# Turning block 0's attention outputs and its inputs of w1 by transposing DMAs instead of on TensorE, with a new order of all operations

## The chip, the cores and the metric

The kernel runs on one core of one Trainium2 chip. The metric is the device time of one execution in microseconds. Before the change it is 1130.92 us, the median of 3 runs that lie between 1130.49 and 1133.29. One further execution was profiled.

## The reference

Two layers, each an attention A and a mixer B, on x of 2048 rows and 512 columns:

```python
x = x + A(layernorm(x));  x = x + B(layernorm(x))      # twice, with the same weights

def A(x, wqkv, wo):       # S = 2048, H = 32 heads, Dh = 16, W = 8 keys, 2 rows apart
    q, k, v = split(x @ wqkv)
    logits = einsum(q, k at rows s, s-2, ..., s-14) * Dh**-0.5     # masked where the row is < 0
    o = softmax(logits) applied to v at the same rows
    return o @ wo

def B(x, w1, w2, w3, w4): # F = 1792
    h  = gelu(layernorm(x) @ w1)
    hs = (h's four groups of 128 columns, shifted by +1, -1, +2, -2 rows) @ w2
    x1 = x + hs
    return x1 + gelu(layernorm(x1) @ w3) @ w4
```

## The kernel before, in words

A layer's 2048 rows are cut into 4 blocks of 512, a block into 4 tiles of 128 rows. A block of a layer is a stage number n from 0 to 7 (the list `lb`; 0 to 3 are layer 0). The work on stage n is:

- `p1_quarters` (n = 0 alone) or `p1_stream(n)`: layer norm, turning the tile into `xt`, and the qkv product. A `p1_stream` is four tiles of three groups of 12 matmuls each (`mm<-wq_hl,xt`).
- `p2(n)`, as `p2_unit(n, ...)`: attention for four quarters of the features, on VectorE (DVE), ScalarE (ACT) and GpSimd (POOL). Each quarter leaves a tile `o`, which is turned into `oT` (lines 1110 to 1113).
- `p3(n)`: oT @ wo, the residual x, the layer norm (`normed`), four tiles turned into `nT` (lines 1170 to 1174), nT @ w1 in four groups of 12 matmuls, gelu, and `h`. In block 0 the wo product is made in four groups, one for each oT as it comes, that add up in four `acc` buffers (`early`); a w1 group needs all four tiles of nT.
- `p4(n)`: h @ w2, the second layer norm, turned into `x2T`; then `p5(n)`: the product with w3, gelu, and the product with w4 in 14 slices.

`small_weight` and `big_four` convert weights meanwhile. Most products are made with each fp32 factor as a high and a low fp16 half, in three matmuls (`HLS`).

A turn has two forms, each of three operations. `turn_pe` transposes four 128x128 pieces in f32 on TensorE (PE) with `ident` into a PSUM buffer `mm`; then ACT writes the high half from PSUM and DVE the low half (`split`). `turn_dma` has ACT write the high half of the tile in SBUF, DVE or POOL the low half beside it (by `OTHER`), both into an `f32` buffer, and SyncE (SP) issues one `dma_start_transpose` of 128 x 8 x 128 fp16, 256 KB. For `o`, whose halves are scaled by `c_o`, the low half on POOL is two instructions. The dictionary `BY_DMA` (line 279) says from which n on a kind of turn goes by DMA: before, p1, p2 and p3 from n = 1 on, p4 from 0 on. Block 0's turns of p2 and p3 therefore are on PE.

What sets the order is a table: `PLACES` holds one number for each of the 3597 operations, and `plan` sorts all operations by it. Each engine issues its own operations in that order (`InOrder`), SP its DMAs too, so an instruction that waits holds up everything behind it on its engine. `OTHER` lists the operations that run on their second choice of engine. Buffers are handed out in the same order. In the profile nearly all instructions carry the one line of `InOrder` (L323), so the groups are told by their tiles' names.

Of the kernel before, what the change touches and what calls it, by code (L numbers as in the profile page):

```python
# [236 lines left out]
class Graph:  # L237
# [3 lines left out]
    def __call__(self, key, alts, r=(), w=(), after=(), xfer=0.0, late=0.0):  # L241
# [30 lines left out]
        for b in o.touch:  # L272
            b.users += 1
            b.left += 1
        self.ops.append(o)
        return o


BY_DMA = {"p1": 1, "p2": 1, "p3": 1, "p4": 0}


def plan(ops, slots):


    pool = {k: list(range(len(v))) for k, v in slots.items()}
# [1150 lines left out]
```

## Time and profile before

| what | value |
|---|---|
| median of 3 runs | 1130.92 us (1130.49 to 1133.29) |
| the profiled execution | 1131.58 us, of which 1129.6 us are its span |
| PE busy | 1113.3 us, 99% of the span |
| DVE busy | 873.4 us, 77% |
| ACT busy | 639.0 us, 57% |
| POOL busy | 456.4 us, 40% |
| granted TensorE clock | 9 tenths or more in all slices |

The times of the trace are counted from the span's start. An arrow `oT<-mm,c_o` reads: written to oT, read from mm and c_o. A busy PE row counts the run of matmuls in it, with its last matmul's own end; successive rows overlap a little, so the distance of two starts is what a group takes. A bracket at a row's end is the idle time of the engine before it and what released it. `SPq` is SP's queue of DMA issues; its rows are as long as the issue takes, not the transfer. Numbers behind a DMA in the list of issues are KB each and the median time from issue to landing.

### The profile page before, as it was taken

Reading aid. Unit: us, or ns where it says so; the run is one execution under the profiler, and the core shown is the slowest. Engines: PE = TensorE matmul, PEld = TensorE weight load, DVE = VectorE, ACT = ScalarE, POOL = GpSimd, SP = SyncE. Lnnn points to the kernel's source line nnn. Section 1 sums busy time; section 2 is a strip of 40 time slices with the busy share of each in tenths; the row PEclk is TensorE's granted clock in tenths of the full one; section 3 lists DMA queues with packets and bytes.
Section 4 is the critical chain, followed back from the end, with each engine's and each line's share of the span. In section 5 each row is a group of like instructions: output and inputs, shape, how many; then the busy total and the mean of one; then the engine's idle time right before and its main releaser. Section 6 shows DMA issues by size and latency. Waiting matters only on the chain.

```text
span 1129.6 us, 15244 instructions
## 1 busy us (share of the span) xinstructions
PE 1113.3 (99%) x5236; PEld 525.5 (47%) x5236; DVE 873.4 (77%) x921; ACT 639.0 (57%) x1222; POOL 456.4 (40%) x554
## 2 busy tenths in 40 slices
PE   8999998999999999999999999999999999999998
PEld 6544444444444444444444444444444444444544
DVE  5999999989898999889889978666878898323212
ACT  5876885267753577364754555564546554655322
POOL 3857754147533470245515343446314341314000
PEclk9999999999999999999999999999999999999999
DMA  7789999988997589864799847974877766425322
GB/s 220 196 219 232 252 277 239 259 230 225 224 243 208 132 207 212 227 155 109 182 207 203 212 111 189 230 175 132 183 191 176 189 145 187 116 66 116 95 85 79
DMA packets 247101, 207.16 MB, mean 183 GB/s; under 512 B 134344, under 2 KB 188616, under 8 KB 247024
## 3 DMA queue, kind: packets, MB, share of 16 engines
q1 hardware_dynamic: 245408, 204.42, 72.1%
q10 hardware_dynamic: 1616, 1.77, 0.6%
q8 instruction: 41, 0.67, 0.3%
q14 instruction: 36, 0.29, 0.1%
HBM read 132.64 MB, written 37.87 MB: 151 GB/s over the span
## 4 chain that ended last, share of the span: by engine, by line
PE 80%; DVE 7%; issue 5%; POOL 4%; ACT 2%; DMA 2%; SPq 1%; ACTq 0%; POOLq 0%; DVEq 0%
PE mm L323 57%; PE acc L323 23%; DVE prod L323 4%; POOL small L323 1%; DVE L L323 1%; SPq L323 1%; ACT junk L323 1%; POOL g L323 1%; DMA nT<-in_A_wqkv_dram 1%; POOL prod L323 1%; DVE inv_p L323 0%; DVE g L323 0%; POOL inv_p L323 0%; DMA nT<-in_A_wo_dram 0%; ACT x L323 0%
## 5 line engine op out<-in xcount | busy, mean ns | idle before, releaser
L323 PE MATMUL acc<-w,g 128*128 128x512 f16 (+1 forms) x1260 | 307.1, 393 | 0.4 <-ACT g L323 0.4
L323 PE MATMUL mm<-nT,w 128*128 128x512 f16 (+1 forms) x1344 | 293.3, 372 | 3.2 <-issue 2.3
L323 PE MATMUL mm<-wq_hl,xt 128*128 128x512 f16 x1008 | 225.4, 379 | 3.5 <-DVE h L323 1.5
L323 PEld LDWEIGHTS <-w 128*128 128x128 f16 x1512 | 141.3, 98 | 158.3 <-issue 8.4
L323 ACT ACTIVATE mm<-mm,s_w 128x512 f32<-128x512 f32 (+1 forms) x144 | 90.1, 628 | 192.5 <-PE mm L323 192.2
L323 PEld LDWEIGHTS <-g 128*128 128x128 f16 x1176 | 114.9, 98 | 137.6 <-issue 0.2
L323 DVE TENSOR_TENSOR prod<-kv,L 128x2048 f32<-128x2048 f32 x64 | 150.4, 2350 | 7.2 <-POOL o L323 5.6
L323 PEld LDWEIGHTS <-xt 128*128 128x128 f16 x1008 | 98.4, 98 | 122.4 <-issue 5.0
L323 DVE TENSOR_REDUCE L<-prod 128x128 f32<-128x2048 f32 x64 | 146.2, 2284 | 1.2
L323 DVE TENSOR_TENSOR prod<-kv,q 128x2048 f32<-128x2048 f32 x58 | 136.6, 2355 | 7.5 <-DMA kv<-kv_d 7.0
L323 DVE TENSOR_TENSOR prod<-prod 128x512 f32<-128x512 f32 (+1 forms) x113 | 115.3, 1023 | 2.9
L323 POOL TENSOR_TENSOR small<-small,nhalf 128x1 f32<-128x1 f32 (+1 forms) x104 | 85.4, 823 | 78.9 <-ACT small L323 76.1
L323 POOL TENSOR_SCALAR small<-small 128x1 f32<-128x1 f32 x131 | 67.8, 520 | 61.5 <-ACT junk L323 25.5
L323 DVE SCALAR_TENSOR_TENSOR g<-mm,c_g,g 128x512 f16<-128x512 f32 x56 | 41.6, 745 | 60.3 <-ACT g L323 60.2
L323 PE MATMUL mm<-nT,w_hl 128*128 128x512 f16 x384 | 86.4, 379 | 0.0
L323 PE MATMUL mm<-w_hl,h 128*128 128x512 f16 x384 | 86.3, 379 | 0.0
L323 POOL TENSOR_TENSOR g<-f,g 128x512 f16<-128x512 f32 x29 | 39.4, 1362 | 89.7 <-ACT g L323 70.4
L323 PE MATMUL mm<-wo_hl,oT 128*128 128x512 f16 x336 | 74.1, 379 | 0.0
L323 POOL TENSOR_TENSOR prod<-prod 128x512 f32<-128x512 f32 (+1 forms) x20 | 30.7, 1534 | 91.5 <-DVE prod L323 88.9
L323 ACT ACTIVATE g<-mm,c_g 128x512 f16<-128x512 f32 x98 | 66.3, 686 | 2.0
L323 PEld LDWEIGHTS <-oT 128*128 128x128 f16 x426 | 41.6, 98 | 49.6 <-issue 0.6
L323 ACT ACTIVATE ev<-mm,s_kv 128x512 f32<-128x512 f32 x56 | 37.9, 682 | 40.8 <-PE mm L323 19.0
(200 smaller groups left out, 1287.5 us busy)
## 6 DMA issues: line engine op xcount, KB each, us to landing
w<-w SPq DMA_DIRECT2D x210, 256.0 KB, 3.3
kv<-kv_d SPq DMA_DIRECT2D x112, 352.0 KB, 5.3
kv_d<-ev SPq DMA_DIRECT2D x112, 128.0 KB, 3.2
w<-in_B_w_dram SPq DMA_DIRECT2D x42, 256.0 KB, 4.5
q_d<-ev SPq DMA_DIRECT2D x28, 256.0 KB, 3.7
w<-g SPq DMA_DIRECT2D x28, 256.0 KB, 4.9
q<-q_d SPq DMA_DIRECT2D x28, 256.0 KB, 4.6
x<-x SPq DMA_DIRECT2D x26, 256.0 KB, 4.8
```

Source lines behind the costliest of these rows:

```text
L323: i = f(*a, **k).ins
```

## The change

`BY_DMA` sends p2's and p3's turns by DMA from n = 0 on. With that the four turns of o into oT and the four of p3's tiles into nT of block 0 use `turn_dma`. The operations stay 3597, since both forms have three. All numbers of `PLACES` and the list `OTHER` are new; of these, a line each is shown. The new table is one line longer, so L323 is L324 in the changed program.

```diff
 PLACES = [int(k) for k in """
-18 67 19 169 24 136 0 1 4 3 13 10 14 5 21 20 33 38 27 22 2 6 7 36
+38 37 39 126 81 83 6 5 1 0 10 9 11 12 16 22 41 35 36 40 7 18 19 24
...
 OTHER = {int(k): 1 for k in """
-21 23 28 42 110 113 114 115 126 128 130 132 148 149 196 205 226 229 230 251 252 255 267 270
+21 28 30 37 44 109 111 112 113 114 124 126 128 132 149 174 196 199 221 227 229 252 254 255
...
-BY_DMA = {"p1": 1, "p2": 1, "p3": 1, "p4": 0}
+BY_DMA = {"p1": 1, "p2": 0, "p3": 0, "p4": 0}
```

PE before, from the last turn of oT to the first w1 group: `ident,o` is a turn of oT, `ident,f` and `ident,prod` are turns of nT, `wq_hl,xt` are groups of `p1_stream` (the first row of each), `acc<-wo_hl,oT` is the last wo group.

```order
L323 MATMUL mm_66<-ident,o_209 128x128 x4
...
L323 MATMUL mm_72<-wq_hl,xt_203 128x512
...
L323 MATMUL acc_211<-wo_hl,oT_218 128x512
...
L323 MATMUL mm_68<-wq_hl,xt_193 128x512
...
L323 MATMUL mm_66<-wq_hl,xt_193 128x512
...
L323 MATMUL mm_70<-ident,f_164 128x128 x4
...
L323 MATMUL mm_72<-wq_hl,xt_193 128x512
...
L323 MATMUL mm_66<-ident,f_168 128x128 x4
...
L323 MATMUL mm_68<-wq_hl,xt_203 128x512
...
L323 MATMUL mm_70<-ident,prod_191 128x128 x4
L323 MATMUL mm_66<-ident,f_176 128x128 x4
...
L323 MATMUL mm_70<-nT_198,w_hl 128x512
```

One qkv group stands between the last turn and the last wo group, and five qkv groups and four turns between that and w1. The same place on PE in the changed program:

```order
L324 MATMUL acc_212<-wo_hl,oT_216 128x512
...
L324 MATMUL acc_212<-wo_hl,oT_218 128x512
...
L324 MATMUL mm_68<-wq_hl,xt_200 128x512
...
L324 MATMUL mm_66<-wq_hl,xt_200 128x512
...
L324 MATMUL mm_72<-wq_hl,xt_203 128x512
...
L324 MATMUL mm_70<-wq_hl,xt_203 128x512
...
L324 MATMUL mm_68<-wq_hl,xt_200 128x512
...
L324 MATMUL mm_66<-wq_hl,xt_203 128x512
...
L324 MATMUL mm_70<-nT_188,w_hl 128x512
```

The last two wo groups stand side by side, and six qkv groups and no turn stand between them and w1. On SP the changed program has these rows there, from the last oT to the four transposes of nT (`xt` are p1's turns, `kv_d`, `q_d` and `x` attention's stores and loads, `w` weights):

```order
L324 DMA_TRANSPOSE oT_218<-f_167 128x8x128
L324 DMA w_183<-in_B_w_dram 128x4x128
L324 DMA_TRANSPOSE xt_200<-f_162 128x8x128
...
L324 DMA_TRANSPOSE xt_203<-f_179 128x8x128
...
L324 DMA w_172<-in_B_w_dram 128x4x128
L324 DMA_TRANSPOSE nT_188<-f_201 128x8x128
L324 DMA_TRANSPOSE nT_188<-prod_198 128x8x128
L324 DMA_TRANSPOSE nT_188<-f_175 128x8x128
L324 DMA_TRANSPOSE nT_188<-f_179 128x8x128
L324 DMA w_0_117<-g_176 128x1024
```

Before, SP had only the transposes of xt in that stretch; four of oT now stand among the work ahead of w1, and four of nT one behind another.

321 rows, old and new, of tables (OTHER, PLACES) are left out of this document.

## The prediction

> **What bounds the kernel now.** I read the page's busy line and chain first, then the busy times by stage, then the waits of TensorE (PE), then the timeline of block 0. The busy line and the chain:
>
> ```profile
> PE 1113.3 (99%) x5236; PEld 525.5 (47%) x5236; DVE 873.4 (77%) x921; ACT 639.0 (57%) x1222; POOL 456.4 (40%) x554
> PE 80%; DVE 7%; issue 5%; POOL 4%; ACT 2%; DMA 2%; SPq 1%; ACTq 0%; POOLq 0%; DVEq 0%
> ```
>
> PE is busy for 99% of the span, so PE work taken away looks like time taken away. The stages say where that holds (columns: length, then busy time of PE, its weight loads, DVE, ACT, POOL; clock; DMA share):
>
> ```profile
> 23.00:124.00 101.00, 98.61 (x426) 49.71 (x425) 98.42 (x93) 79.07 (x184) 73.59 (x74) 1.00 0.81 216
> 124.00:180.00 56.00, 53.67 (x262) 25.67 (x261) 55.25 (x71) 45.01 (x87) 35.48 (x47) 1.00 1.01 261
> 180.00:320.00 140.00, 136.17 (x588) 64.64 (x587) 130.15 (x149) 79.36 (x158) 60.48 (x68) 1.00 0.90 235
> 320.00:1095.00 775.00, 774.96 (x3680) 354.78 (x3679) 570.41 (x571) 417.53 (x752) 278.29 (x347) 1.00 0.69 167
> ```
>
> From 320 us on PE never stops. From 23 to 180 us, where the whole change lies, DVE is as full as PE: 98.42 of 101 and 55.25 of 56. Two engines bound that stage, and the DMA share is 1.01 in its second part. PE's waits from 130 to 320 us (total, times, longest):
>
> ```profile
> PE mm L323 <- issue: 2.3, 1, 2.3
> PE mm L323 <- DVE h L323: 1.5, 2, 1.3
> PE mm L323 <- ACT junk L323: 1.1, 3, 0.8
> PE mm L323 <- ACT ev L323: 0.7, 1, 0.7
> ```
>
> The 2.3 is the start of p5(0), the first large PE stage, which waits for its input x2T.
>
> **What the change removes.** One turn on PE, in the timeline, and all sixteen transposes of the four oT:
>
> ```profile
> 71.48 0.60 PE L323 MATMUL mm<-ident,o 128*128 128x128 f32 x4
> 71.92 5.34 PE L323 MATMUL mm<-wq_hl,xt 128*128 128x512 f16 x24
> L323 PE MATMUL mm<-ident,o x16: 272/273/273, 71.5 to 125.4; 128*128 128x128 f32 x16
> ```
>
> The next matmul starts 71.92 - 71.48 = 0.44 us after the turn does: a turn takes 0.44 of PE's row (each 0.273 overlaps its neighbour). Eight turns are 8 x 0.44 = 3.5 us. That is the most that PE's own work can give.
>
> **What it adds on the path.** Block 0's path, on PE:
>
> ```profile
> 125.08 0.60 PE L323 MATMUL mm<-ident,o 128*128 128x128 f32 x4
> 125.51 2.75 PE L323 MATMUL mm<-wq_hl,xt 128*128 128x512 f16 x12
> 128.10 2.75 PE L323 MATMUL acc<-wo_hl,oT 128*128 128x512 f16 x12
> 145.44 2.75 PE L323 MATMUL mm<-nT,w_hl 128*128 128x512 f16 x12
> 156.13 2.75 PE L323 MATMUL mm<-nT,w_hl 128*128 128x512 f16 x12
> 161.45 7.93 PE L323 MATMUL mm<-w_hl,h 128*128 128x512 f16 x36
> 169.22 7.95 PE L323 MATMUL mm<-wq_hl,xt 128*128 128x512 f16 x36
> 179.47 1.79 PE L323 MATMUL mm<-nT,w 128*128 128x384 f16 x10 [2.29 <-issue]
> ```
>
> A group of 12 matmuls takes 128.10 - 125.51 = 2.59. In order these are: the last turn of oT, a qkv group, the last wo group, the first and last of four w1 groups, p4(0), three more qkv groups, p5(0). Its other engines, each row from its engine's timeline:
>
> ```profile
> 123.99 0.77 POOL L323 TENSOR_TENSOR o<-prod 128x256 f32<-128x256 f32 x1 [0.67 <-DVE prod L323]
> 125.72 0.69 ACT L323 ACTIVATE oT<-mm,c_o 128x512 f16<-128x512 f32 x1 [1.36 <-PE mm L323]
> 127.23 0.74 DVE L323 SCALAR_TENSOR_TENSOR oT<-mm,c_o,oT 128x512 f16<-128x512 f32 x1
> 140.47 0.81 ACT L323 ACTIVATE prod<-x,small 128x512 f32<-128x512 f32 x1
> 160.67 0.74 DVE L323 SCALAR_TENSOR_TENSOR h<-mm,c_h,h 128x512 f16<-128x512 f32 x1
> ```
>
> So the last o is ready at 123.99 + 0.77 = 124.76, the last oT at 127.97, the last normalized tile of p3(0) at 140.47 + 0.81 = 141.28, the last h at 161.41. The turns that replace PE's already run in later blocks; their steps by group (busy, mean ns):
>
> ```profile
> L323 ACT ACTIVATE f<-o,c_o 128x512 f16<-128x512 f32 x23 | 16.4, 717 | 26.9 <-DVE o L323 13.4 <-POOL o L323 9.9 <-DMA w<-w 3.5
> L323 DVE SCALAR_TENSOR_TENSOR f<-o,c_o,f 128x512 f16<-128x512 f32 x14 | 12.2, 868 | 12.7 <-ACT f L323 12.7
> L323 POOL TENSOR_TENSOR f<-o,f 128x512 f16<-128x512 f32 x9 | 12.9, 1432 | 0.8
> L323 POOL TENSOR_SCALAR o<-o,c_o 128x512 f32<-128x512 f32 x10 | 11.0, 1098 | 37.4 <-ACT f L323 31.0 <-ACT prod L323 6.5
> L323 ACT ACTIVATE f<-f 128x512 f16<-128x512 f32 x45 | 28.2, 627 | 1.0
> L323 DVE TENSOR_TENSOR f<-f,f 128x512 f16<-128x512 f32 x27 | 18.3, 687 | 10.9 <-ACT f L323 10.8
> ```
>
> and their transposing DMA, on SP's timeline and as the median from issue to landing:
>
> ```profile
> 125.63 1.28 SPq L323 DMA_TRANSPOSE xt<-f  x1
> 176.14 1.28 SPq L323 DMA_TRANSPOSE nT<-prod  x1
> oT<-f SPq DMA_TRANSPOSE x23, 4.8
> ```
>
> The row at 176.14 feeds p5(0), which starts at 179.47: 3.33 us from the start of the issue to the use. I take 3.33, since that row lies nearest in time and has the same size; 4.8 is the upper end; the lower is the 1.28 of the issue alone.
>
> - Last oT (halves on ACT and DVE in the new code): 124.76 + 0.72 + 0.87 + 3.33 = 129.7. With four turns gone PE would be there at 128.10 - 4 x 0.44 = 126.3, so it now waits about 3.4 us. Behind that wait stand all later PE groups, and behind this DMA on SP one load and the next xt, issued at about 126.4 + 1.28 + 0.5 and landed 3.33 later, 131.5, before PE needs it at 129.7 + 2.6 = 132.3.
> - x, statistics and normalizing take 141.28 - 128.10 = 13.2 from the start of the last wo group, now to 142.9. The last turn of nT adds 0.63 + 0.69 + 3.33 = 4.65: nT at 147.6. PE, after the wo group and six qkv groups (7 x 2.59 = 18.1) and some tiny matmuls, comes at 148.0, so nT just fits. w1 starts at 148.0, where it was 145.44.
> - The four w1 groups stand together now: 4 x 2.59 to 158.4. The last h came 161.41 - 158.72 = 2.7 after the last w1 group: 161.1, and p4(0) at 161.2 (was 161.45). p5(0) comes 179.47 - 161.45 = 18.0 later: 179.2. So 0.3 is won, and PE, 3.5 us lighter, waits at the last wo and again at x2T.
>
> Behind p5(0) PE's remaining work is the same in both orders. Of the 4 to 6 us of waits there, the 1.5 for h may shrink, as DVE has about 1 us less to do for the turns (two lo halves go to POOL, 1.10 + 1.43 each, where POOL has 35.48 of 56): between 0 and 1.5, I take 0.5. ACT's halves change by under 0.05 each (0.69 to 0.72): nothing.
>
> The Trainium skill, page "VectorE: DVE Perf Modes", section "The three transpose paths", gives 390 ns for a 128x128 transpose on TensorE and 1309 ns on the DMA crossbar, and its section "Rules for kernel authors" prefers TensorE wherever PSUM will do as the destination. That speaks against this change. The trace agrees in direction (0.44 against 3.33), but here the engine that the rule prefers has no idle time after 320 us. By the page's 1.31 the last oT would land at 127.7 and PE alone would set the start of w1, 146.0; p5(0) at 177.2 would then make 1131.58 - 2.3 - 0.5 - 0.66, about 1128.1.
>
> **SP.** Eight issues of 1.28 are 10.2 us more on SP's queue, four of them (5.1) ahead of the last oT. SP's largest idle times from 60 to 145 us, by what they waited for:
>
> ```profile
> SPq L323 <- POOL small L323: 2.8, 2, 1.6
> SPq L323 <- ACT f L323: 2.5, 5, 0.6
> SPq L323 <- ACT junk L323: 1.4, 2, 0.9
> SPq L323 <- ACT ev L323: 1.4, 2, 0.8
> ```
>
> These alone are 8.1 us, more than the 5.1, but they are waits in order at the head of the queue, so not all can be filled. I take them as enough; the other end is a rival.
>
> **Sum.** 1131.58 (profiled execution; the median of the runs is 1130.92, 0.66 less) - 0.3 - 0.5 = 1130.8; to the median, 1130.1. A measurement of this kernel can tell about 0.3% from no change, 3.4 us: 1127.5 to 1134.3 is "the same".
>
> **The rivals.**
> 1. *PE alone sets it* (faster). If the new order brings the last o and the layer norm earlier, so that no wait replaces the turns, 3.5 stay won, with the 0.5 behind: 1126.9 (1125.9 with all 1.5). For it: PE's 99%. Against it: DVE's 98.42 of 101 and 55.25 of 56 allow some 3.3 us in all. 0.20.
> 2. *Slow landing*. Both turns land after 4.8, not 3.33: last oT at 131.2, nT at 142.9 + 1.5 + 0.63 + 0.69 + 4.8 = 150.5, p5(0) 31.2 later (179.2 - 148.0) at 181.7, or +2.2: 1133.1. For it: the DMA share of 1.01. Against: the row of 3.33 lies in that stage. 0.13.
> 3. *SP's queue* (slower). If SP's idle takes up none of the four issues ahead of the last oT, it lands 5.1 later, 134.8; w1 then starts at 134.8 + 18.3 = 153.1, p5(0) at 184.3, or +4.8: 1135.7. It decides for slower once more than about 3.5 of the 5.1 is not absorbed. For it: SP's issues stand nearly end to end there. Against: the 8.1 of idle. 0.22.
>
> That the turns don't move is excluded: the changed program has eight transposing DMAs more on SP ahead of p4(0), and eight rows less on PE.
>
> **How the numbers follow.** The saving given back as waits has 0.45, at 1130.1, with 1128 to 1132.5 as its own range (DVE's 0 to 1.5, and 1 to 2 us at the landing). The range reaches from 1126.5 (most of rival 1) to 1136.0 (past the middle of rival 3) and leaves out about 0.18. Faster: rival 1, 0.20. Slower: rival 3, 0.22. The rest, 0.58, is the same.
>
> **What would show it.** Right: PE's busy sum about 3.5 lower; a PE wait of 2 to 4 us for a DMA into oT at the last wo group near 130; w1 near 148; p5(0) near 179, again after a wait of over 2 us; nothing waiting after 320. Wrong: no wait at the last wo group and p5(0) by 177 (rival 1); oT transposes on SP issued more than 3 us after their lo half, and p5(0) past 182 (rival 3); or new waits in p2 and p5 behind 180 us, of which the order alone tells no price.

## The result, and the profile after

The changed kernel takes 1144.6 us (median of 4 runs, 1144.09 to 1148.45) beside 1131.82 for the kernel before in the same comparisons (4 runs): ratio 1.012, 95% interval 1.0094 to 1.0146. It is slower by 12.8 us; forecast were 1130.1 us, 1126.5 to 1136.0. The profiled execution has 1144.62 us, its span is 1142.4.

The busy line of the changed kernel:

```profile
PE 1116.9 (98%) x5204; PEld 524.4 (46%) x5204; DVE 881.5 (77%) x911; ACT 637.2 (56%) x1230; POOL 484.3 (42%) x559
```

PE has 32 matmuls less, and yet is busy for longer: 1116.9 against 1113.3. The turns took 8 x 0.44 = 3.5 us with them, so some 7.1 us of busy time were added: the same matmuls took longer (those of `mm<-nT,w` with 384 columns 326 ns on the mean before, 345 after). PE's idle time rose from 1129.6 - 1113.3 = 16.3 to 25.5, by 9.2. That is the whole account: - 3.5 + 7.1 + 9.2 = 12.8. By stage (columns as in the stage rows of the prediction; the last three are clock, DMA share and GB/s):

```profile
23.00:124.00 101.00, 96.04 (x394) 47.32 (x393) 98.13 (x94) 75.74 (x179) 69.64 (x70) 0.97 0.85 216
124.00:180.00 56.00, 50.63 (x229) 22.60 (x228) 50.35 (x63) 43.05 (x87) 45.12 (x47) 0.97 1.04 252
180.00:320.00 140.00, 133.63 (x567) 63.45 (x566) 124.66 (x140) 78.28 (x158) 69.22 (x80) 0.98 0.95 236
320.00:1095.00 775.00, 773.64 (x3664) 353.63 (x3665) 587.42 (x572) 419.63 (x762) 292.32 (x343) 1.00 0.68 170
```

All but some 1.3 us of the added idle time lies before 320 us, and the granted clock, 1.00 in all four stages before, is 0.97 to 0.98 there. PE's waits from 130 to 320 us:

```profile
PE mm L324 <- DMA nT<-f: 5.8, 2, 4.0
PE acc L324 <- DMA w<-in_B_w_dram: 2.0, 2, 1.1
PE acc L324 <- DMA oT<-f: 1.2, 1, 1.2
PE mm L324 <- DMA xt<-prod: 1.0, 1, 1.0
```

and the longest one before 130, which the kernel before does not have:

```profile
PE mm L324 <- ACT w_hl L324: 4.0, 1, 4.0
```

All but 0.5 us of the waits from 130 to 320 us are for a DMA now. The marks of the forecast, on PE's timeline (last wo group, first w1 group, p4(0), p5(0)):

```profile
134.18 2.76 PE L324 MATMUL acc<-wo_hl,oT 128*128 128x512 f16 x12 [1.23 <-DMA oT<-f]
155.03 11.98 PE L324 MATMUL mm<-nT,w_hl 128*128 128x512 f16 x48 [1.86 <-DMA nT<-f]
169.57 7.93 PE L324 MATMUL mm<-w_hl,h 128*128 128x512 f16 x36
190.43 6.56 PE L324 MATMUL mm<-nT,w 128*128 128x384 f16 x24 [3.98 <-DMA nT<-f]
```

Forecast were 129.7, 148.0, 161.2 and 179.2: late by 4.5, 7.0, 8.4 and 11.2 us. The rest of the span, from p5(0) on, is 1142.4 - 190.43 = 952.0, where 1129.6 - 0.8 - 179.2 = 949.6 were forecast: 2.4 more.

### The profile page after: what moved, and what is told of

Read it like the earlier page. It is cut to its first block, busy times and chain, and to the rows that moved or that the text cites. A ratio compares the mean times of both kernels' runs of the same rounds, so it can differ in the third digit from the quotient of the medians.

```text
span 1142.4 us, 15185 instructions
## 1 busy us (share of the span) xinstructions
PE 1116.9 (98%) x5204; PEld 524.4 (46%) x5204; DVE 881.5 (77%) x911; ACT 637.2 (56%) x1230; POOL 484.3 (42%) x559
## 4 chain that ended last, share of the span: by engine, by line
PE 75%; POOL 4%; ACT 3%; DMA 3%; DVE 3%; issue 1%; SPq 1%; POOLq 0%; DVEq 0%; ACTq 0%
PE mm L324 51%; PE acc L324 24%; POOL small L324 2%; DVE prod L324 1%; DMA w<-in_B_w_dram 1%; SPq L324 1%; DMA kv_d<-ev 1%; ACT f L324 1%; ACT junk L324 1%; DMA nT<-f 1%; POOL g L324 1%; DMA w<-w 0%; DVE f L324 0%; POOL o L324 0%; ACT mm L324 0%
## 5 line engine op out<-in xcount | busy, mean ns | idle before, releaser
L324 PE MATMUL acc<-w,g 128*128 128x512 f16 (+1 forms) x1260 | 307.2, 394 | 2.0 <-DMA w<-in_B_w_dram 2.0
L324 PE MATMUL mm<-nT,w 128*128 128x512 f16 (+1 forms) x1344 | 296.7, 375 | 4.4 <-DMA nT<-f 4.0
L324 PE MATMUL mm<-wq_hl,xt 128*128 128x512 f16 x1008 | 227.4, 383 | 4.4 <-ACT ev L324 1.3
L324 PEld LDWEIGHTS <-w 128*128 128x128 f16 x1512 | 142.2, 98 | 162.2 <-issue 12.1
L324 ACT ACTIVATE mm<-mm,s_w 128x512 f32<-128x512 f32 (+1 forms) x144 | 89.7, 628 | 202.3 <-PE mm L324 202.0
L324 PEld LDWEIGHTS <-g 128*128 128x128 f16 x1176 | 114.8, 98 | 137.6
L324 DVE TENSOR_TENSOR prod<-kv,L 128x2048 f32<-128x2048 f32 x64 | 150.5, 2354 | 11.8 <-POOL o L324 6.9
L324 PEld LDWEIGHTS <-xt 128*128 128x128 f16 x1008 | 99.4, 99 | 127.0 <-issue 8.6
L324 DVE TENSOR_TENSOR prod<-kv,q 128x2048 f32<-128x2048 f32 x58 | 138.9, 2396 | 12.4 <-DMA kv<-kv_d 8.9
L324 DVE TENSOR_REDUCE L<-prod 128x128 f32<-128x2048 f32 x64 | 146.1, 2282 | 1.1
L324 DVE TENSOR_TENSOR prod<-prod 128x1024 f32<-128x1024 f32 (+2 forms) x117 | 128.9, 1107 | 6.9 <-ACT prod L324 4.2
L324 POOL TENSOR_TENSOR small<-small,nhalf 128x1 f32<-128x1 f32 (+1 forms) x104 | 93.6, 903 | 82.4 <-ACT small L324 79.9
L324 POOL TENSOR_SCALAR small<-small 128x1 f32<-128x1 f32 (+1 forms) x120 | 59.7, 500 | 88.2 <-ACT junk L324 58.7
L324 PE MATMUL mm<-nT,w_hl 128*128 128x512 f16 x384 | 87.6, 384 | 1.9 <-DMA nT<-f 1.9
L324 PE MATMUL mm<-w_hl,h 128*128 128x512 f16 x384 | 85.6, 379 | 0.0
L324 DVE SCALAR_TENSOR_TENSOR g<-mm,c_g,g 128x512 f16<-128x512 f32 x56 | 41.5, 745 | 56.2 <-ACT g L324 56.1
L324 POOL TENSOR_TENSOR g<-f,g 128x512 f16<-128x512 f32 x34 | 50.1, 1480 | 73.5 <-ACT f L324 59.8
L324 PE MATMUL mm<-wo_hl,oT 128*128 128x512 f16 x336 | 74.0, 379 | 0.0
L324 ACT ACTIVATE g<-mm,c_g 128x512 f16<-128x512 f32 x98 | 65.9, 684 | 1.8
L324 PEld LDWEIGHTS <-oT 128*128 128x128 f16 x426 | 41.4, 98 | 51.2 <-DMA oT<-f 1.7
L324 PEld LDWEIGHTS <-w_hl 128*128 128x128 f16 x384 | 37.8, 99 | 48.5 <-issue 2.5
L324 PEld LDWEIGHTS <-h 128*128 128x128 f16 x384 | 37.6, 98 | 44.6
```

What stands on the lines that cost most here:

```text
L324: i = f(*a, **k).ins
```

## The experiments

Theory A: the turns themselves cost, by the landing of their DMAs and by SP's queue. Theory B: the new order costs, whichever engine turns. All times are medians of 4 to 10 runs; ratios are to the kernel before in the same comparison.

**Turns or order.** Four kernels separate them: the old order with all eight turns by DMA, the new order with them on PE, the old order with oT's turns alone, and with nT's alone.

```diff
 # e1 (before.py); e4 changes only "p2", e18 only "p3"
-BY_DMA = {"p1": 1, "p2": 1, "p3": 1, "p4": 0}
+BY_DMA = {"p1": 1, "p2": 0, "p3": 0, "p4": 0}
 # e2 (after.py)
+for _k, _v in ((404, 286.6), (405, 286.7), (406, 286.8), (415, 400.6),
...
+    PLACES[_k] = _v
-BY_DMA = {"p1": 1, "p2": 0, "p3": 0, "p4": 0}
+BY_DMA = {"p1": 1, "p2": 1, "p3": 1, "p4": 0}
```

> The order of before is kept, number for number, and the eight turns of block 0 go by DMA: each turn's three operations take the three places of the old turn. Theory A (the turns cost: the landing of each DMA, and SP's queue): the loss comes with the turns alone, so this is above 1140 us. Theory B (the new order costs: the loads of w1 stand late on SP, PE waits 4.0 us for them near 82 to 86 us, and the clock falls to 0.50 after each long wait): without the new order there is no such wait, and this is between 1130 and 1138 us, the upper end because wo follows each turn closely in this order.

Measured: 1154.81 us, ratio 1.0204 (1.0189 to 1.0219).

> The order of the changed kernel, with the eight turns of block 0 back on TensorE; the three operations of a turn stand together, near the place of the first one, because only four PSUM buffers are there. Theory A (turns cost): most of the 12.8 us comes back, 1130 to 1135 us. Theory B (order costs): the wait of 4.0 us for w1's sum of squares and the slow clock behind it stay, so 1138 to 1146 us.

Measured: 1161.64 us, 1.0265 (1.025 to 1.028).

> The order of before, with the four turns of o into oT by DMA and those of nT on TensorE. Theory A: about half of the loss, 1136 to 1140 us, since these turns are on the path once for the last oT. Theory B: 1130 to 1135 us.

Measured: 1144.64 us, 1.0119 (1.0102 to 1.0136).

> The order of before, with the four turns of nT by DMA and those of o on TensorE. If the costs of the two kinds of turn add up (e1 cost 23.2 us, e4 alone 13.0), 1140 to 1143 us. If they don't add (one long wait hides another), 1144 us or more, or under 1138.

Measured: 1142.35 us, 1.0098 (1.0083 to 1.0113).

Theory B falls: in the old order the turns alone cost 23.2 us, and the two kinds add up (13.0 + 11.1 = 24.1). Theory A as stated falls as well: the new order without its DMA turns is the slowest of all (though e2 also moves the three operations of each turn together and takes two entries out of `OTHER`, so it is not the order alone). The new order fits the new turns and takes back 1154.8 - 1144.6 = 10.2 us of what they cost in the old one. What they cost there is on PE's list of waits of e1, up to 320 us:

```profile
PE mm L323 <- DMA nT<-f: 9.2, 1, 9.2
PE mm L323 <- DMA xt<-f: 8.9, 4, 5.2
PE acc L323 <- DMA oT<-f: 4.0, 1, 4.0
```

Only 13.2 of these 22.1 us are for the newly turned tiles. The other 8.9 are for xt, p1's tiles, whose turns were by DMA already: they now stand behind the new ones on SP. The kernel before waited 0.7 for them.

**SP's queue by itself.** The kernel before, with small stores that nobody waits for at the eight places; 16 of them in e5, 32 in e17; in e16 16, with 16 loads of x issued by ACT.

```diff
 # e5 and e16; e17 has range(32) and range(4)
+    spare = [dram.tile([P, 64], F16, name=f"spare{k}") for k in range(16)]
+    EXTRA = (406, 417, 459, 470, 992, 1002, 1012, 1022)
     for o in plan(op.ops, slots):
         o.fn()
+        if o.seq in EXTRA:
+            for _ in range(2):
+                Y.dma_start(spare.pop(), wq.t[:, :64])
 # e16, e6, e7 (in dma2, used by load_x for blocks 2 and 3)
-                Y.dma_start(out(par), in_(par))
+                (q or Y).dma_start(out(par), in_(par))
```

> The kernel before, with its turns on TensorE, and 16 small stores of a part of wq_hl to spare DRAM, which nobody waits for, two at each of the eight places where an old turn had its last operation. They add SP issues alone (16 of 0.5 to 0.6, some 9 us; what the eight transposing DMAs add is 10.2), and no landing that anything needs. Theory SP (SP's queue is full from 60 to 160 us, and each issue put in delays all that stand behind it): 1137 to 1145 us. Theory landing (the path is longer because the turned tiles land later): within 3 us of before.

Measured: 1138.66 us, 1.0065 (1.0042 to 1.0088).

> The kernel before with 32 spare issues, four at each of the eight places, 17.5 us of SP. Theory SP full: each us of issue costs what it cost in e5 (6.8 for 8.8) or more, since there is no slack left: 1144 to 1150 us. If SP still had room and e5 met one unlucky place: under 1142 us.

Measured: 1147.36 us, 1.0145 (1.013 to 1.016).

> The kernel before with the 16 spare issues of e5 on SP, and 16 loads of x off SP, issued by ACT. SP's queue is then about as long as before. Theory SP (length of the queue): the loss of e5 goes, 1130 to 1134 us. Theory place (each spare issue delays what stands right behind it, and the loads taken off stood elsewhere): 1136 us or more.

Measured: 1138.18 us, 1.0058 (1.0041 to 1.0075).

Issues alone cost 0.65% for 8.8 us of SP and 1.45% for 17.2: 7.4 and 16.4 us, some 0.8 to 0.95 us for each us of issue, with no landing that anybody needs. The stores' own data, 16 KB each, did not fill the DMA engines: their busy share from 60 to 180 us is 0.94 in the kernel before, 0.92 in e5 and 0.86 in e17. (In the changed kernel it is 0.99; whether its transfers also slow each other down, these runs don't separate.) PE's wait for xt shows the way, in the kernel before, in e5 (its profiled execution is its slowest, 1143.37 us) and in e17:

```profile
PE mm L323 <- DMA xt<-f: 0.7, 1, 0.7
```

```profile
PE mm L323 <- DMA xt<-f: 4.7, 4, 2.9
```

```profile
PE mm L323 <- DMA xt<-f: 6.9, 5, 3.1
PE mm L323 <- ACT ev L323: 4.1, 3, 2.2
```

The second row of e17 is next in the line: ACT waits for buffers of ev, which SP's stores empty. From 40 to 180 us ACT waits in the kernel before, and in e17:

```profile
ACT ev L323 <- DMA kv_d<-ev: 4.4, 3, 3.0
ACT ev L323 <- DMA q_d<-ev: 2.4, 1, 2.4
```

```profile
ACT ev L323 <- DMA kv_d<-ev: 9.2, 6, 3.3
ACT ev L323 <- DMA q_d<-ev: 6.9, 4, 3.3
```

e16 says that it isn't the length of the queue: with as much taken off it as was put on, the loss stayed. That leaves the place: an issue ahead of a transfer on the path delays that transfer, and room made elsewhere is not passed on. Tile by tile this is not shown for e16: its wait for xt is only 1.7 us, yet its p4(0) starts at 167.95, 6.5 later than in the kernel before.

**Taking work off SP.**

> The changed kernel, with the loads of x for p1 of blocks 2 and 3 (8 operations, 16 issues of 0.6, 9.6 us) issued by ACT in place of SP, at the same places of the order. Theory SP: the 9.6 us come off the full queue, and most of the loss comes back: 1132 to 1139 us. Theory landing: SP's length matters little, 1142 us or more. ACT takes the issues in (75.74 of 101 us busy).

Measured: 1146.75 us, 1.0138 (1.0117 to 1.016).

> The kernel before with the same 16 issues by ACT. If SP's queue has the whole say, there is a gain here as well, at most the 6 us that PE waits from 124 to 320 us: 1126 to 1131 us. If SP only counts once it is overfull, no change within 2 us.

Measured: 1132.24 us, 1.0003 (0.9993 to 1.0013).

The loads of x were no part of the path in either kernel: neither gained. In e6 the last wo group starts at 134.22, where it started at 134.18.

**The slow clock.** In e8 warm-up matmuls fill three of PE's waits.

```diff
+    BUSY = {157: 30, 1026: 16, 1088: 30}
     for o in plan(op.ops, slots):
+        for _ in range(BUSY.get(o.seq, 0)):
+            T.matmul([t for t in o.touch if t.kind == "mm"][0].t[:, :2 * P], warm[:, :P], warm, start=True, stop=True)
         o.fn()
```

> The changed kernel with 30, 16 and 30 matmuls of warm-up data (128x256, results overwritten) on PE ahead of the three matmuls at which it idles longest (w1's sum of squares, first w1 group, p5(0)); they need nothing, so they run within the idle time. If the slow clock behind each long wait is lost time of its own: no 0.50 in the granted clock there, and 3 to 7 us less, 1138 to 1142 us. If the time that the slow clock takes is made up by shorter waits behind it: within 2 us of 1144.6.

Measured: 1141.24 us, 1.0083 (1.0064 to 1.0101); the interval still touches that of the changed kernel, though each of its four runs is faster than each of the four there. The granted clock of the changed kernel at the first of these waits and the third (length, PE busy ... clock, DMA share):

```profile
82.00:86.00 4.00, 0.58 (x3) 0.09 (x1) 3.97 (x4) 1.48 (x1) 3.92 (x3) 1.00 0.75 238
86.00:90.00 4.00, 3.42 (x9) 1.54 (x10) 4.00 (x4) 3.93 (x9) 4.00 (x4) 0.54 0.93 232
90.00:94.00 4.00, 4.00 (x13) 1.51 (x12) 4.00 (x3) 0.56 (x2) 4.00 (x2) 0.61 0.87 231
190.00:194.00 4.00, 3.57 (x12) 1.70 (x13) 3.97 (x2) 1.12 (x1) 2.16 (x2) 0.50 1.02 267
194.00:198.00 4.00, 4.00 (x17) 2.08 (x16) 3.86 (x5) 2.02 (x4) 0.00 (x0) 0.81 1.05 314
```

and of e8, at the same places of its own timeline:

```profile
86.00:88.00 2.00, 2.00 (x22) 1.81 (x20) 1.58 (x1) 2.00 (x5) 2.00 (x2) 1.00 0.79 262
88.00:90.00 2.00, 2.00 (x13) 0.98 (x12) 1.72 (x3) 1.94 (x5) 2.00 (x3) 1.00 1.03 202
194.00:196.00 2.00, 2.00 (x14) 1.23 (x13) 1.90 (x4) 1.71 (x3) 0.00 (x0) 1.00 1.02 333
```

At 0.54, 0.61, 0.50 and 0.81 the 16 us of these rows lose some 4 x (0.46 + 0.39 + 0.50 + 0.19) = 6.2 us; with the shorter spell behind the wait ahead of w1 this is about the 7.1 of the account above. With PE kept busy the clock stays at 1.00 at these places, and about half of that comes back (3.4). PE's waits for xt are 6.2 us in e8, where they were 2.0, though 1.98 of that stands ahead of the first warm-up and can't come from it. The third warm-up also cost time of its own: it ran to 192.14, though the last turn ahead of p5(0) was issued at 186.26 and so was due near 189.5, by the 3.26 us from issue to use in the changed kernel (an estimate).

**Single delays on the path.** The changed kernel's last o comes at 128.07 and not at 124.76, with two halves of oT ahead of it on POOL; the last of w1's four loads stands behind the first turn on SP (78.09, the load 79.68, its use 84.52); a weight's low half stands ahead of a root of p4(0). Each was taken away alone.

```diff
 # e3: two loads of w1 behind the second one        # e10: the weight's half behind the root
+for _k, _v in ((154, 272.3), (153, 272.6)):        +for _k, _v in ((267, 742.5),):
+    PLACES[_k] = _v                                 +    PLACES[_k] = _v
 # e9: seqs 416 and 458 out of OTHER
-... 413 414 416 458 463 467 473
+... 413 414 463 467 473
```

> The changed kernel with two of the four loads of w1 moved ahead on SP, to stand behind the second one; nothing else. Theory A: SP's queue and the landings of the turns set the later path anyway, so this stays within 3 us of 1144.6. Theory B: the wait of 4.0 us before the sum of squares of w1 and the some 3 us of slow clock behind it go, and with them 4 to 7 us: 1137 to 1141 us.

Measured: 1147.22 us, 1.0133 (1.0101 to 1.0164).

> The changed kernel with the two low halves of oT that OTHER puts on POOL (1.64 + 1.47 us there, the later pair ahead of the last o) back on DVE (0.87 each). Theory POOL (the last o comes at 128.07 and not at 124.76, since POOL's queue holds it up): last o some 2 to 3 us earlier, last wo group at 131 to 132 in place of 134.18, and 2 to 4 us less: 1141 to 1143 us. Theory SP (the transposes would wait on SP's queue anyway): last wo group within 1 us of 134.18, 1144 to 1147 us.

Measured: 1142.83 us, 1.0107 (1.0082 to 1.0133).

> The changed kernel with one low half of a weight (POOL, w and g, 179.26 to 183.15) moved behind p4(0)'s last layer norm on POOL. Theory POOL: the root that waits for it comes some 2 us earlier, PE idles 2 us less ahead of p5(0), below the length that brings the clock to 0.50, so p5(0) at 188 to 189 in place of 190.43 and 3 to 5 us less: 1140 to 1142 us. Theory SP: no change beyond 2 us.

Measured: 1145.32 us, 1.011 (1.009 to 1.0131).

None is told from no change. Two of them show why. In e3 the wait ahead of w1's sum of squares fell from 4.00 to 1.17 us, but PE's wait for an xt just before it grew from 0.97 to 3.23, since that xt's turn is issued behind the two loads, at 75.41 and not at 73.28:

```profile
79.77 5.35 PE L326 MATMUL mm<-wq_hl,xt 128*128 128x512 f16 x24 [3.23 <-DMA xt<-f]
```

e9's POOL has the last o two us earlier (124.44 + 1.52 = 125.96; it was 126.22 + 1.85):

```profile
124.44 1.52 POOL L324 TENSOR_TENSOR o<-prod 128x256 f32<-128x256 f32 x2
```

Its DVE has the low half at 128.86:

```profile
128.11 0.75 DVE L324 SCALAR_TENSOR_TENSOR f<-o,c_o,f 128x512 f16<-128x512 f32 x1 [0.89 <-ACT f L324]
```

But SP comes to that turn at 131.42 (130.95 in the changed kernel):

```profile
126.11 0.93 SPq L324 DMA_DIRECT2D kv_d<-ev  x1
127.15 0.54 SPq L324 DMA_DIRECT2D q<-q_d  x1
128.16 2.65 SPq L324 DMA_DIRECT2D kv_d<-ev  x4
130.85 0.47 SPq L324 DMA_DIRECT2D kv_d<-x  x1
131.42 1.30 SPq L324 DMA_TRANSPOSE oT<-f  x1
```

and PE at 134.63, where it was 134.18:

```profile
134.63 2.76 PE L324 MATMUL acc<-wo_hl,oT 128*128 128x512 f16 x12 [1.54 <-DMA oT<-f]
```

Six stores and one load stand between the third and the fourth turn on SP, and the tile waits 2.6 us for them.

**Several at once, and shorter issues.** e11 is e9 and e10 together, e12 adds e8's warm-up; e13 is e9 and e6, e14 is all four; e15 has plain copies for the eight transposing DMAs, so that block 0's oT and nT aren't turned.

> Both edits, the low halves on DVE and the weight's low half behind the root. Theory POOL: the sum of the two, 1137 to 1140 us. Theory SP: 1142 us or more.

Measured: 1145.35 us, 1.0117 (1.0093 to 1.0141).

> Both edits, and the warm-up matmuls ahead of the three longest waits of PE. Theory POOL and clock: 1133 to 1138 us. What is left over the 1131.8 of before is then SP's longer queue, which none of these touches; theory SP: over 1138 us.

Measured: 1143.87 us, 1.0113 (1.009 to 1.0135).

> The changed kernel with both reliefs that did nothing alone: the low halves of oT on DVE, and the 16 loads of x by ACT. Theory two queues (the last oT needs POOL for o and SP for the issue; whichever is relieved, the other is late next): the last oT is issued near 128 to 129 and the last wo group starts at 131 to 132.5, where each alone left it at 134.2 to 134.6; the time 1136 to 1141 us. Theory SP alone: e6 had relieved it already, so as there, 1144 to 1147 us.

Measured: 1147.23 us, 1.0134 (1.0116 to 1.0151).

> The same, with the weight's low half behind p4(0)'s root, and the warm-up matmuls. Theory two queues: each edit now counts, 1133 to 1138 us. If it stays over 1140, a further queue (ACT, which issues the loads now, or DVE, 98 of 101 us busy) holds the same path.

Measured: 1145.75 us, 1.0121 (1.0103 to 1.0139).

> The changed kernel with plain copies of the same 256 KB in place of the eight transposing DMAs of block 0; the data then isn't turned, everything else runs as it did. A plain issue takes some 0.55 us on SP and not 1.28, 5.8 us less in all. Theory SP's issue time: 1138 to 1142 us. If the transposes cost by their landing and by where they wait in the queue, and not by the length of their issue: within 2 us of 1144.6.

Measured: 1144.03 us, 1.0115 (1.01 to 1.013).

My theory of two queues in series falls too: e13 puts the last wo group at 136.02. SP stood idle there, without an issue from 123.66 to 126.85, ahead of the third turn, whose low half DVE ended at 126.83, and everything behind it moved along:

```profile
122.36 1.30 SPq L324 DMA_DIRECT2D kv<-kv_d  x2
126.85 1.27 SPq L324 DMA_TRANSPOSE oT<-f  x1
```

A turn that has to wait for its low half holds the queue, full or not. And e15 shows that the 1.28 us of the issue isn't the matter either: with shorter ones the last wo group of e15 starts at 132.1, w1 at 152.46 and p5(0) at 188.59, each some 2 us sooner, but PE's wait ahead of p5(0) is 5.27 there, where it was 3.98, and the median moved by 0.6 us. None of the eighteen is faster than the kernel before.

## Why the prediction was wrong

Two steps failed, and two costs had no term: SP's room was taken as enough, the last o's time was taken over from the old order, and neither the slow clock behind PE's waits nor a stretched issue on SP was priced.

*PE saves 3.5 us.* Right, and worth nothing, as forecast: it comes back as waits. (The sums of rivals 2 and 3 leave out the 0.5 that the main sum takes off behind p5(0); with it they are 1132.6 and 1135.2.)

*The two landings on the path.* The mechanism was right: PE waits for oT at the last wo group, then for nT, then for x2T. Issue to use is 134.18 - 130.95 = 3.2 us, where 3.33 was taken. What was wrong is when the issue starts. I put it at the end of the low half, 124.76 + 0.72 + 0.87 = 126.35; it was 130.95. Of these 4.6 us, 3.3 are the later o (128.07), which I took over from the old order, and 1.3 SP. e9 took 2.1 of the 3.3 away, and SP's part grew to 2.6.

At w1 a size was off as well. The forecast had nT just fit; PE waited 1.86 us for it. The first of its four issues holds SP for 3.24 us, where the other three take 1.26 to 1.29, and these 2 us by themselves are as long as the wait:

```profile
145.33 3.24 SPq L324 DMA_TRANSPOSE nT<-f  x1
```

It takes 2.15 to 4.55 us in e3, e6 and e8 to e14 too, but 1.25 and 1.30 in e1 and e18, and 0.62 as e15's plain copy, where PE does not wait for nT at w1. What stretches it no run shows.

*SP: "I take them as enough".* This step failed. I read 8.1 us of SP's waits from the four largest rows of that list as room for 5.1 us of issues. The timeline of SP's queue shows no such room: its rows from 60 to 120 us, cut at the ends, add up to 54.5 of 60 us in the kernel before, and the rest are gaps of mostly 0.05 to 0.1 us between one issue and the next. The longest is this one, of 0.74:

```profile
111.02 1.81 SPq L323 DMA_DIRECT2D kv_d<-ev  x2
113.57 1.28 SPq L323 DMA_TRANSPOSE xt<-f  x1
114.95 0.52 SPq L323 DMA_DIRECT2D q_d<-ev  x1
```

The list has single waits of up to 1.6 us, and the timeline has no gap of that length up to 145 us, so the list's sum was not idle time. The second error is in what I counted: only the four issues ahead of the last oT, and only what they do to oT. By e1, 8.9 of 22.1 us are waits for xt, and in the changed kernel up to 1.6 of the 4.0 for w1 is of the same kind: the last load stands behind the first turn, which holds SP from 78.09 on. The rest goes with the new order, which has the issues of w1's loads between 67.45 and 80.42 and not between 65.04 and 68.08; e1, in the old one, has no such wait. Rival 3 named the place, and priced 4.8 us on one transfer. By e5 and e17 issues alone cost 0.8 to 0.95 us per us, so 10.2 us of them would make 8 to 10. That is an estimate for the old order; how much of the 12.8 is issue and how much is landing in the new one stays open, since every delay that was taken away left another behind it. Rows above show which for e3, e9, e13 and e15; for the others it isn't shown.

*Waits priced at their length.* PE's waits of 4.0 and 3.98 us cost it time behind them as well, some 6.2 of the 7.1 us, and e8 got back 3.4. The forecast had no term for this, though it had PE wait 3.4 us at the last wo group. The longest wait of the old kernel, 2.29, leaves no trace in the clock (below), so its profile gave no hint. The Trainium skill, page "TensorE: Matmul & The Clock Gate", section "Part 1: The HAM clock gate (the "warmup" mystery)", says that the array drops to half clock after an idle window of about 3.4 us and needs as long of work to come back. The trace agrees with the drop for the two long waits: 0.50. The way back took longer, some 6 and 5 us.

*p4(0) to p5(0), 18.0.* It was 20.9. A wait of 1.0 for xt is in it, and a root of its layer norm that POOL reached late; e10 shortened the stretch to 191.16 - 171.46 = 19.7, but not the total.

*The range.* It ended at 1136.0, since no case had SP's delay on more than one transfer, or the clock.

## What to carry to other kernels

A step that is moved to a DMA takes room on the queue that issues it, and what pays is all that stands behind it there. Read the queue's own timeline, issue by issue, and not the sum of its waits; where the rows stand end to end, as here, a us of issue put ahead of a transfer on the path cost 0.8 to 0.95 us of time, and relief at another place didn't return it. A wait of PE can cost more than its length: behind some waits of 2 to 4 us the clock stood near half for 3 to 6 us, behind others it did not.

## What the hardware showed that was not expected

The granted clock fell to half even after shorter waits. In the changed kernel PE is idle from 136.78 + 15.70 = 152.48 to 155.03 but for two tiny matmuls, and the clock is 0.57 behind that:

```profile
136.78 15.70 PE L324 MATMUL mm<-wq_hl,xt 128*128 128x512 f16 x72
152.78 0.39 PE L324 MATMUL mm<-small,ones 128*128 128x4 f32 x2 [0.30 <-ACT junk L324]
```

```profile
154.00:158.00 4.00, 2.97 (x8) 1.04 (x9) 3.97 (x3) 0.65 (x2) 4.00 (x3) 0.57 0.85 249
```

In e8 PE waits 2.27 us ahead of a group of 36:

```profile
179.40 9.63 PE L324 MATMUL mm<-wq_hl,xt 128*128 128x512 f16 x36 [2.27 <-DMA xt<-prod]
```

These 36 matmuls take 9.63 us, where 7.93 to 7.95 is normal, at this clock:

```profile
180.00:182.00 2.00, 2.00 (x9) 0.76 (x7) 2.00 (x2) 1.58 (x4) 2.00 (x1) 0.69 0.94 194
182.00:184.00 2.00, 2.00 (x6) 0.70 (x5) 2.00 (x2) 0.19 (x1) 1.90 (x5) 0.50 1.04 315
```
In the same run 24 matmuls behind a wait of 1.98 us take 7.04 us, where 5.34 is normal, at 0.59 and 0.56 from 78 to 82 us:

```profile
77.81 7.04 PE L324 MATMUL mm<-wq_hl,xt 128*128 128x512 f16 x24 [1.98 <-DMA xt<-f]
```

The kernel before had a wait of 2.29 without any such mark (1.00 from 178 to 182):

```profile
178.00:182.00 4.00, 2.53 (x16) 1.59 (x17) 3.97 (x2) 0.73 (x2) 3.51 (x2) 1.00 0.83 230
```

Nor did the clock fall behind the 3.23 us of e3: its 24 matmuls take 5.35 us (the row at 79.77), at 1.00 from 76 to 84. So the length of the wait alone does not decide here: 1.98 was enough once, and 3.23 was not. What decides no run shows.

POOL's instructions can be stretched by DVE's large ones. The same subtraction on the changed kernel's POOL, twice:

```profile
174.69 1.16 POOL L324 TENSOR_TENSOR g<-w,g 128x512 f16<-128x512 f32 x1
180.03 3.12 POOL L324 TENSOR_TENSOR g<-w,g 128x512 f16<-128x512 f32 x1
```

The second starts while DVE multiplies two inputs from SBUF for 2.28 us:

```profile
179.85 2.28 DVE L324 TENSOR_TENSOR prod<-kv,q 128x2048 f32<-128x2048 f32 x1
```

It is longer by 1.96, nearly what is left of that instruction (182.13 - 180.03 = 2.1). The one other such subtraction in this run that starts within a DVE row of this kind, at 318.7, takes 3.07; one that starts ahead of it, at 152.3, keeps its 1.16. The Trainium skill, page "SBUF — State Buffer", section "SBUF: two separate sides", tells of a port pair that the two share, which one of them holds for a whole instruction; the rows agree. Work moved from DVE to POOL should be priced at such a row.
